# A transformer block on one core: image 0's output projection moved ahead of three V tiles and of image 1's P V, with P moves on a second queue

## The chip, the core and the metric

The kernel runs on one core of a Trainium2 chip. A core has a matrix engine (TensorE, PE), three engines for elementwise work (VectorE or DVE, ScalarE or ACT, GpSimd or POOL), SyncE (SP), which here only issues transfers, and 16 DMA engines that carry out what SP, ScalarE and GpSimd issue on their queues. Engines run their own instruction streams in order and wait for one another on semaphores. The metric is the device time of one execution in microseconds; less is better.

## The reference

Two images of 256 tokens, width 1152, two heads of 576, MLP width 4608, all bf16:

```
mod = (silu(c) @ w_mod).reshape(B, 6, 1, D)
shift_a, scale_a, gate_a, shift_m, scale_m, gate_m = [mod[:, i] for i in range(6)]
h = layernorm(x) * (1 + scale_a) + shift_a
q, k, v = split(h @ wqkv)                       # B, N, H, Dh
attn = softmax(einsum('bqhd,bkhd->bhqk', q, k) * Dh ** -0.5)
a = einsum('bhqk,bkhd->bqhd', attn, v).reshape(B, N, D) @ wo
x = x + gate_a * a
h2 = layernorm(x) * (1 + scale_m) + shift_m
out = x + gate_m * (gelu(h2 @ w_fc1) @ w_fc2)
```

## The kernel before

**Tiles.** The 512 tokens are four tiles t of 128; tiles 0 and 1 are image 0, tiles 2 and 3 image 1. The width is nine chunks of 128 (kt, or g for the attention output), or three column groups ci of 384. Everything lies in one SBUF array, "arena", cut by hand into regions that several buffers share in turn, and in eight PSUM banks.

**Stages on TensorE**, in order: modulation and LayerNorm 1, K, Q, the scores S of each image b and head h (index b*2+h), V (`v_proj(t, ci)`, nine matmuls of 384 columns, L1035), P V, the output projection (`wo_tile(t)`, three tiles of nine matmuls, L1164), FC1 (`fc1_tile(f, tok0, ntok)`, 36 rows f of the MLP width, nine matmuls of ntok columns each, L1205), FC2. A tile is evicted from PSUM by ScalarE or VectorE: `v_ev<t>_<ci>` on ScalarE, `wo_t1_<t>_<ci>` on VectorE (L1174), `gelu_<f>_<tok0>` on ScalarE (L1212).

**Softmax and the turn of P.** For each score block ScalarE makes the exponentials (`sexp`) and normalises (`spn`, L1026), VectorE turns P in 32 by 32 blocks (`PT_turn<idx>`, L1028), and four transfers of 32 KB put the turned blocks in place (`mv_pt<idx>_<a>`, L1030). Head 0 is idx 0 and 2, head 1 idx 1 and 3. Before, all sixteen are issued by SP.

**P V.** `pv(b, h)` (L1141) makes four chunks of one image and head in 16 matmuls of 256 columns and needs `PT` of that block; the chunk that holds the end of head 0 and the start of head 1 (g = 4) is made by `pv_halves()` (L1130) for both images, and needs all four. Results go to OT by `OT_ev<b>_<g>` and `OT_ev_4`. OT lies in the region of HX, which V's matmuls read. V itself lies in the region that later holds H2T, the normalised input of the MLP.

**The second LayerNorm.** After `wo_t1`, GpSimd adds x (`wo_x1`), VectorE takes statistics (`bn_ln2`), GpSimd finishes them (`rstd_ln2`, `nmr2`), ScalarE normalises (`xn2_<t>`, L1181), VectorE turns the tile (`h2turn_<t>`), four transfers move it (`mv_h2_<t>_<a>`), and nine pieces `h2T_<t>_<kt>` on ScalarE (L1199) and VectorE (L1202) apply scale and shift. FC1's first tiles use only the tokens that are ready: some rows f run first for 128 tokens (f < NF) or 256 (f < F0) and come back for the rest.

**Order.** TensorE's and SP's streams are in the order in which the program makes them; those of ScalarE, VectorE and GpSimd come from a list scheduler held by hand-written lists (`S.in_order`). The gates need a chain of their own on VectorE: `ga_<b>_<kt>` (16 operations of 1.41 us), which ends in `ga_t1`, and goes through a DRAM scratch to GA. `rows()` makes the MLP's shift and scale on TensorE, read by VectorE as `mt_0`, `mt_1`, `sc1m`. SP's large loads are W_O (`ld_wo`), the gate's and W_fc1's blocks of 512 columns (`ld_wfc1_<q>`, nine blocks in a ring of five slots), the MLP gate's weight (`ld_gm`) and four parts of W_fc2.

The order of the stage in question before:

```
        for t in range(1, 4):
            for ci in range(NCH):
                v_proj(t, ci)
...
        pv(0, 0)
        pv(1, 0)
        rows()
        pv_halves()
        pv(0, 1)
        pv(1, 1)
...
        wo_tile(0)
```

Of the kernel before, what the change touches and what calls it, by code (L numbers as in the profile page):

```python
# [515 lines left out]
NCH = 3  # L516
F0 = 20
NF = 10
KC = 5
# [33 lines left out]
def build_kernel(nc, x, c, wqkv, wo, w_mod, w_fc1, w_fc2, out):  # L553
# [5 lines left out]
    with (  # L559
# [70 lines left out]
        GM = [sb(o + 18432, 2304) for o in (O_A, O_C)]  # L630
        XN2 = [sb(O_R + 4 * W1 - (i + 1) * 2304, 2304) for i in range(4)]
        ACCA = sb(O_R, FG * 8, F32).rearrange("p (b d) -> p b d", b=2)
# [94 lines left out]

        def wfc1_load(q, k0=0, k1=KT):
            dma(WFC1[q % 5][:, k0:k1, :], wfc1_v[:, k0:k1, q * 512:(q + 1) * 512], (k1 - k0) * P * 1024, "ld_wfc1_%d_%d" % (q, k0), run=1024)

# [274 lines left out]
        def s_and_softmax(b, h):  # L1005
# [29 lines left out]
        def v_proj(t, ci):  # L1035
            bank = v_banks[v_rr[0] % 4]
            v_rr[0] += 1
# [89 lines left out]

        PVB = [(6, 7, 1, 6), (5, 2, 7, 5)]

        def pv_halves():  # L1130
            S.unit("pe", 4 * c_mm(256) + 100.0, "PV_halves")
            for b in range(2):
                for kjt in range(2):
                    for q in range(4):
                        r = slice(32 * q, 32 * q + 32)
                        mm(psum[r, b * 256:b * 256 + 256], V[:, 2 * b + kjt, 512 + 32 * q:544 + 32 * q],
                           PTS[b * 2 + q // 2][:, kjt], b == 0 and kjt == 0, b == 1 and kjt == 1, skip_group_check=True,
                           tile_position=(0, 32 * q))
            copy_on("act", OT[:, 4, :], ps32(0), 512, False, "OT_ev_4")

        def pv(b, h):  # L1141
# [13 lines left out]
        act(1500, lambda e: e.activation(out=SUMS[:, 0:1], in_=NHALF, func=ACTF.Gelu_apprx_tanh), [NHALF], [SUMS[:, 0:1]], "gelu_tab")  # L1155
        acc = [2, 3, 4, 6, 5, 7, 0, 1]
        acc_rr = [0]

        def acc_bank():
            b = acc[acc_rr[0] % len(acc)]  # L1160
            acc_rr[0] += 1
            return b

        def wo_tile(t):  # L1164
            b = t // 2
            for ci in range(NCH):
                S.unit("pe", KT * c_mm(CH), "wo_%d_%d" % (t, ci))
                o = ps32(acc_bank(), 0, CH)
                for g in range(KT):
                    mm(o, OT[:, g, t * 128:(t + 1) * 128], WO[:, g, ci * CH:(ci + 1) * CH], g == 0, g == KT - 1)  # L1170
                ga = GA[b][:, ci * CH:(ci + 1) * CH]
# [12 lines left out]

        TURNED = {0: H2F[3], 1: H2F[2], 2: XN2[0], 3: XN2[1]}

# [4 lines left out]
        def xn2_move(t):  # L1191
            b, b0 = t // 2, 0
            for a in range(4):
                dma(H2F[t][:, 288 * a:288 * a + 288], TURNED[t][32 * a:32 * a + 32, :], P * 576, "mv_h2_%d_%d" % (t, a), run=576, eng="act" if t in (0, 3) and a > 1 else "sp")
            for kt in range(KT):
                dst = H2T[:, kt, 4 * t:4 * t + 4, :]
                s1, s2 = SC1M[:, kt * 2 + b:kt * 2 + b + 1], SHM[:, kt * 32 + b:kt * 32 + b + 1]
                if kt < 7 if t == 0 else (kt > 6 if t == 1 else kt % 3 == 2):
                    act(330, lambda e, dst=dst, s1=s1, s2=s2: e.activation(out=dst, in_=dst, func=ACTF.Identity, scale=s1, bias=s2),  # L1199
# [5 lines left out]
        def fc1_tile(f, tok0, ntok):  # L1205
# [3 lines left out]
            for kt in range(KT):  # L1209
                mm(o, WFC1[q % 5][:, kt, (f % 4) * 128:(f % 4) * 128 + 128], H2T[:, kt, tok0 // 32:(tok0 + ntok) // 32, :], kt == 0, kt == KT - 1)  # L1210
            dst = GT[f][:, tok0:tok0 + ntok]
# [51 lines left out]
        wo_tile(2)  # L1263
# [12 lines left out]
        for f in (1, 2):  # L1276
            fc1_tile(f, 128, 256)
        for f in (1, 2):
            fc1_tile(f, 384, 128)
        fc1_tile(0, 256, 256)  # L1280
        for f in range(3, NF):
            fc1_tile(f, 128, 384)
        for f in range(NF, F0):
            fc1_tile(f, 256, 256)
        for f in range(F0, JT):
            if f % 4 == 0:
                if 24 <= f < 32:
                    wfc2_load(f // 4 - 5)
                wfc1_load(f // 4)
# [6 lines left out]
        for t in range(4):  # L1296
# [4 lines left out]
            for (c0, c1) in pieces:  # L1301
# [4 lines left out]
                for j in js:  # L1306
# [6 lines left out]

        S.n_other_dma_sems = 16
        small = ["ga_%s" % n for n in ("mv%d_1", "mv%d_2", "mv%d_3", "add%d_1", "add%d_3", "add%d_2", "bf%d", "t%d")]
        S.in_order("dve", ["ga_%d_%d" % (b, kt) for kt in range(3) for b in range(2)] + ["ga_0_%d" % kt for kt in range(3, 7)]
                   + ["smax_0", "snb_0", "ga_0_7", "sri_0", "ga_0_8", "smax_2", "snb_2", "PT_turn0", "smax_1", "snb_1", "sri_2", "ga_T0",
                      "smax_3", "snb_3", "sri_1", "PT_turn2", "ga_red0", "PT_turn1", "sri_3"] + [n % 0 for n in small] + ["PT_turn3"]
                   + ["ga_1_%d" % kt for kt in range(3, KT)] + ["ga_T1", "ga_red1"] + [n % 1 for n in small] + ["OT_ev0_7", "mt_0", "mt_1", "OT_ev1_7"])
        S.in_order("act", ["sexp_0_0", "sexp_0_1", "qk_ev8", "spn_0_0", "spn_0_1", "v_ev0_0", "sexp_2_0", "sexp_2_1", "sexp_1_0", "sexp_1_1", "v_ev0_1",  # L1320
                           "spn_2_0", "spn_2_1", "spn_1_0", "spn_1_1", "v_ev0_2", "sexp_3_0", "sexp_3_1", "v_ev1_0", "spn_3_0", "spn_3_1", "v_ev1_1", "v_ev1_2"])
        S.in_order("act", ["OT_ev0_0", "OT_ev0_2", "OT_ev1_0", "OT_ev1_2", "OT_ev_4", "OT_ev0_5", "OT_ev1_5", "gelu_tab", "xn2_0"])
        S.in_order("pool", ["wo_x1_0_0", "wo_x1_0_1", "wo_x1_0_2", "wo_x1_1_0", "rstd_ln2_0", "nmr2_0", "wo_x1_1_1", "wo_x1_1_2", "rstd_ln2_1", "nmr2_1", "wo_x1_2_0", "wo_x1_2_1", "wo_x1_2_2",
                            "wo_x1_3_0", "rstd_ln2_2", "nmr2_2", "wo_x1_3_1", "wo_x1_3_2", "rstd_ln2_3"])
# [55 lines left out]
```

## Time and profile before

| | |
|---|---|
| runs | 240.17 us (median of 3; 240.11 to 241.54) |
| the profiled execution | 240.14 us, of which the span of the profile is 238.2 us |
| TensorE busy in the span | 233.2 us, 1781 matmuls |
| VectorE, ScalarE, GpSimd busy | 125.7, 73.4, 23.4 us |
| granted TensorE clock | 1.0 |
| HBM read | 50.15 MB |

All times in this document that are positions are microseconds from the start of the span. The profile gives each engine's work in order of time (the timeline), in groups of like instructions by line, and in 40 equal slices; the chain that ended last, followed back from the end; the transfers, with the time from their issue to their landing; and what each engine waited for. "PE" is TensorE's matmuls, "PEld" its weight loads, "SPq" and "ACTq" the instructions by which SP and ScalarE issue a transfer. The chain's shares say what the end of the kernel depended on; an engine that is off the chain may wait at no cost.

### The profile page before, as it was taken

The numbers are of one execution on the slowest core, as the hardware profiler recorded it, in microseconds if no ns is written. First come the engines' busy times: TensorE is split into PE (matmuls) and PEld (weight loads), VectorE is DVE, ScalarE is ACT, GpSimd is POOL, SyncE is SP. The second block draws the span as 40 slices with busy tenths as digits, with TensorE's granted clock in tenths as the row PEclk, the third lists the DMA queues.
The fourth block names the chain that finished last, engine by engine and source line by source line (L and its number), as shares of the span: only waits on it lengthen the run. The fifth ranks groups of instructions, "written<-read, shape, count | busy, mean of one in ns | idle before, by whom it ended". The sixth has DMA issues, their size and how long they took to land.

```text
span 238.2 us, 4224 instructions
## 1 busy us (share of the span) xinstructions
PE 233.2 (98%) x1781; PEld 149.0 (63%) x1781; DVE 125.7 (53%) x233; ACT 73.4 (31%) x159; POOL 23.4 (10%) x48
## 2 busy tenths in 40 slices
PE   6899999999999999999999999999999999999995
PEld 2688844466667656989668644444665656656664
DVE  2654399979997699853299997000111111111112
ACT  4940540458535326767333333333000000000000
POOL 1300000000201467510000001100000000000000
DMA  6999999999999852849799999980000000000000
GB/s 219 361 372 391 352 391 391 394 412 410 316 355 356 259 190 63 256 112 318 242 385 371 390 354 379 392 313 2 3 17 17 19 17 17 17 22 23 22 20 18
DMA packets 36173, 53.31 MB, mean 224 GB/s; under 512 B 5371, under 2 KB 21627, under 8 KB 36155
## 3 DMA queue, kind: packets, MB, share of 16 engines
q1 hardware_dynamic: 34976, 51.85, 62.4%
q0 software_dynamic: 432, 0.89, 1.0%
q10 hardware_dynamic: 747, 0.31, 0.5%
q8 instruction: 14, 0.23, 0.4%
q14 instruction: 4, 0.03, 0.0%
HBM read 50.15 MB, written 1.19 MB: 216 GB/s over the span
## 4 chain that ended last, share of the span: by engine, by line
PE 95%; DMA 3%; SPq 1%; DVE 0%; issue 0%
PE psum L704 94%; DMA arena<-in_w_mod_dram 3%; SPq L685 1%; PE psum L707 0%; DVE arena L845 0%; DVE arena L1310 0%; DVE arena L1311 0%; DVE arena L833 0%
## 5 line engine op out<-in xcount | busy, mean ns | idle before, releaser
L704 PE MATMUL psum<-arena 128*128 128x384 bf16 (+10 forms) x1744 | 231.5, 302 | 2.1 <-POOL arena L732 1.5
L704 PEld LDWEIGHTS psum<-arena 128*128 128x128 bf16 (+3 forms) x1744 | 147.1, 97 | 84.8 <-issue 3.1
L1310 DVE TENSOR_TENSOR arena<-psum,arena 128x384 f32<-128x384 f32 (+2 forms) x13 | 6.8, 526 | 74.7 <-PE psum L704 74.7
L1212 ACT ACTIVATE arena<-psum 128x256 bf16<-128x256 f32 (+3 forms) x59 | 24.7, 430 | 41.2 <-PE psum L704 41.1
L699 ACT ACTIVATE arena<-psum 128x512 bf16<-128x512 f32 (+5 forms) x35 | 18.6, 561 | 30.8 <-PE psum L704 30.8
L1070 DVE SCALAR_TENSOR_TENSOR arena<-arena 128x1152 f32<-128x1152 bf16 x16 | 22.3, 1412 | 0.2
L1105 DVE SCALAR_TENSOR_TENSOR arena<-arena 128x1152 f32<-128x1152 bf16 x16 | 21.4, 1414 | 0.0
L685 POOL DMA_DIRECT2D dit_scratch<-arena x6 | 3.5, 584 | 99.5 <-DVE arena L1087 53.8
L754 DVE BATCH_NORM_STATS2 arena<-arena 128x6 f32<-128x384 f32 (+1 forms) x18 | 9.5, 549 | 4.1 <-DMA arena<-in_x_dram 3.9
L1175 POOL TENSOR_TENSOR arena<-arena 128x384 f32<-128x384 f32 x12 | 10.8, 912 | 5.9 <-DVE arena L1174 5.9
L1181 ACT ACTIVATE arena<-arena 128x1152 bf16<-128x1152 f32 x4 | 5.4, 1345 | 9.7 <-POOL arena L1180 6.4
L1174 DVE TENSOR_TENSOR arena<-psum,arena 128x384 f32<-128x384 f32 x12 | 6.5, 555 | 2.5 <-PE psum L704 2.5
L701 DVE CAST arena<-psum 128x512 bf16<-128x512 f32 x8 | 5.4, 684 | 4.1 <-PE psum L704 4.1
L1311 DVE TENSOR_TENSOR arena<-arena 128x384 bf16<-128x384 f32 (+2 forms) x13 | 6.9, 528 | 0.4
L1202 DVE TENSOR_SCALAR arena<-arena 128x128 bf16<-128x128 bf16 x21 | 5.4, 326 | 3.0 <-DMA arena<-arena 3.0
L1199 ACT ACTIVATE arena<-arena 128x128 bf16<-128x128 bf16 x15 | 6.2, 482 | 0.1
L1189 DVE STREAM_TRANSPOSE arena<-arena 128x1152 bf16<-128x1152 bf16 x4 | 5.5, 1377 | 1.1 <-ACT arena L1181 1.1
L1102 DVE TENSOR_SCALAR arena<-arena 128x1152 f32<-128x1152 bf16 x2 | 1.6, 818 | 7.6 <-DMA arena<-in_w_mod_dram 7.6
L1021 ACT ACTIVATE arena<-psum,arena 128x256 bf16<-128x256 f32 x8 | 3.7, 469 | 2.4 <-DVE arena L1018 1.9
L758 POOL TENSOR_TENSOR arena<-arena 128x1 f32<-128x1 f32 x6 | 3.4, 566 | 3.8 <-DVE arena L757 3.6
L1026 ACT ACTIVATE arena<-arena 128x256 bf16<-128x256 bf16 x8 | 3.6, 501 | 0.1
L1017 DVE TENSOR_REDUCE arena<-psum 128x2 f32<-128x512 f32 x4 | 2.8, 690 | 1.5 <-PE psum L704 1.3
(64 smaller groups left out, 62.0 us busy)
## 6 DMA issues: line engine op xcount, KB each, us to landing
arena<-in_w_fc_dram SPq DMA_DIRECT2D x4, 2592.0 KB, 17.2
arena<-in_w_fc_dram SPq DMA_DIRECT2D x8, 1152.0 KB, 12.0
arena<-in_w_mod_dram SPq DMA_DIRECT2D x6, 864.0 KB, 11.4
arena<-in_w_mod_dram SPq DMA_DIRECT2D x3, 1728.0 KB, 20.4
arena<-in_wqkv_dram SPq DMA_DIRECT2D x9, 288.0 KB, 8.0
arena<-in_wqkv_dram SPq DMA_DIRECT2D x1, 2592.0 KB, 18.2
arena<-in_wo_dram SPq DMA_DIRECT2D x1, 2592.0 KB, 9.8
arena<-in_w_mod_dram SPq DMA_DIRECT2D x1, 2592.0 KB, 11.0
```

What stands on the lines that cost most here:

```text
L685: return S.op(eng, 500.0 if eng == "sp" else 150.0, lambda e: e.dma_start(dst, src), reads=[src], writes=[dst], name=name, dma_bytes=nbyte ...
L699: act(c_act(n), lambda e: e.activation(out=dst, in_=src, func=ACTF.Copy), [src], [dst], name)
L704: S.instr(lambda e: e.matmul(o, lhsT=l, rhs=r, start=st, stop=sp, **kw), reads=[l, r], writes=[o])
L754: dve(550, lambda e, s=s, o=o: e.bn_stats(out=o, in_=s), [s], [o], "bn_%s_%d" % (tag, ci))
L1070: ga_units[(b, kt)] = dve(150 + FG * 1.1, lambda e, o=o, w=w, s1=s1: e.scalar_tensor_tensor(out=o, in0=w, scalar=s1, in1=o, op0=ALU.mult, ...
L1105: u = dve(1300, lambda e, o=o, w=w, s1=s1: e.scalar_tensor_tensor(out=o, in0=w, scalar=s1, in1=o, op0=ALU.mult, op1=ALU.add), [w, s1, o], ...
L1174: dve(550, lambda e, o=o, ga=ga, x1c=x1c: e.tensor_tensor(out=x1c, in0=o, in1=ga, op=ALU.mult), [o, ga], [x1c], "wo_t1_%d_%d" % (t, ci))
L1175: S.op("pool", 930, lambda e, xs=xs, x1c=x1c: e.tensor_tensor(out=x1c, in0=x1c, in1=xs, op=ALU.add), reads=[x1c, xs], writes=[x1c], name=" ...
L1199: act(330, lambda e, dst=dst, s1=s1, s2=s2: e.activation(out=dst, in_=dst, func=ACTF.Identity, scale=s1, bias=s2), [dst, s1, s2], [dst], " ...
L1212: act(c_act(ntok), lambda e: e.activation(out=dst, in_=o, func=ACTF.Gelu_apprx_tanh), [o], [dst], "gelu_%d_%d" % (f, tok0))
L1310: dve(c_dve_psum32(w), lambda e, o=o, gm=gm, t1=t1: e.tensor_tensor(out=t1, in0=o, in1=gm, op=ALU.mult), [o, gm], [t1], "fc2_t1_%d_%d" % ( ...
L1311: dve(c_dve_32(w), lambda e, t1=t1, x1c=x1c, ost=ost: e.tensor_tensor(out=ost, in0=t1, in1=x1c, op=ALU.add), [t1, x1c], [ost], "fc2_out_%d ...
```

## The change

Image 0's six W_O tiles come ahead of three of V's tiles (3_0, 2_2, 3_2) and of image 1's P V. Both heads of image 0 are multiplied before `rows`. The moves of P for head 1 (idx 1 and 3) are issued by ScalarE instead of SP. The result of `pv_halves` gets a buffer of its own, OT4, where Q4B was, so that it doesn't overwrite HX; two turned tiles of the second LayerNorm get room too. W_fc1's ring has four slots instead of five, block 3 is loaded in one piece, and blocks 2 and 3 are issued after the moves of tiles 0 and 1. FC1's split is another: 3 rows start with 128 tokens, 8 with 256, 3 with 384, and from row 14 on all 512 go at once (before: 10 rows at 128, 10 at 256, 512 from row 20). The PSUM banks and the hand-written orders of ScalarE and VectorE follow; ScalarE does 20 of the 36 `h2T` pieces instead of 15.

```diff
-F0 = 20
-NF = 10
+NF = 3
+F1 = 11
+F0 = 14
...
-        WFC1 = [wmat(o, 512) for o in (O_A, O_A + 9216, O_C, O_C + 9216, O_R + 3 * W1)]
+        WFC1 = [wmat(o, 512) for o in (O_A, O_A + 9216, O_C, O_C + 9216)]
...
+        OT4 = sb(O_Q4B, 1024)
...
-                dma(PPF[idx][:, 128 * a:128 * a + 128], flat[32 * a:32 * a + 32, :], P * 256, "mv_pt%d_%d" % (idx, a), run=256)
+                dma(PPF[idx][:, 128 * a:128 * a + 128], flat[32 * a:32 * a + 32, :], P * 256, "mv_pt%d_%d" % (idx, a), run=256, eng="act" if h else "sp")
...
-        PVB = [(6, 7, 1, 6), (5, 2, 7, 5)]
+        PVB = [(6, 5, 1, 2), (1, 2, 0, 7)]
...
-            copy_on("act", OT[:, 4, :], ps32(0), 512, False, "OT_ev_4")
+            copy_on("act", OT4, ps32(0), 512, False, "OT_ev_4")
...
-            for i, eng in ((0, "act"), (1, "dve" if h else "act")):
+            for i, eng in ((0, "act" if h or not b else "dve"), (1, "dve" if b and h else "act")):
...
-                dma(H2F[t][:, 288 * a:288 * a + 288], TURNED[t][32 * a:32 * a + 32, :], P * 576, "mv_h2_%d_%d" % (t, a), run=576, eng="act" if t in (0, 3) and a > 1 else "sp")
+                dma(H2F[t][:, 288 * a:288 * a + 288], TURNED[t][32 * a:32 * a + 32, :], P * 576, "mv_h2_%d_%d" % (t, a), run=576, eng="act" if t > 2 and a > 1 else "sp")
...
         v_proj(0, 2)
-        for t in range(1, 4):
-            for ci in range(NCH):
-                v_proj(t, ci)
-        wfc1_load(2)
+        for ci in range(NCH):
+            v_proj(1, ci)
+        v_proj(2, 1)
+        v_proj(3, 1)
+        v_proj(2, 0)
         gate_load(1)
-        wfc1_load(3, 0, 7)
         pv(0, 0)
-        pv(1, 0)
+        pv(0, 1)
         rows()
         pv_halves()
-        pv(0, 1)
-        pv(1, 1)
...
         wo_tile(0)
+        wo_tile(1)
+        v_proj(3, 0, 7)
+        v_proj(2, 2, 6)
+        v_proj(3, 2, 5)
+        pv(1, 0)
+        pv(1, 1)
         xn2_turn(0)
         xn2_move(0)
-        wo_tile(1)
+        wfc1_load(2)
         xn2_turn(1)
         xn2_move(1)
-        wfc1_load(3, 7, KT)
-        wfc1_load(4)
+        wfc1_load(3)
         wo_tile(2)
...
-        fc1_tile(0, 128, 128)
-        for f in range(NF, F0):
+        for f in range(NF, F1):
             fc1_tile(f, 0, 256)
+        for f in range(F1, F0):
+            fc1_tile(f, 0, 384)
         mlp_gate(last_h2T[0])
...
+        for f in range(NF):
+            fc1_tile(f, 128, 384)
+        for f in range(NF, F1):
+            fc1_tile(f, 256, 256)
+        for f in range(F1, F0):
+            fc1_tile(f, 384, 128)
```

In the built program ScalarE's stream from `v_ev1_0` on is: v_ev1_0, mv_pt1_0, spn_3_0, mv_pt1_1, spn_3_1, mv_pt1_2, v_ev1_1, mv_pt1_3, v_ev1_2, v_ev2_1, mv_pt3_0 to mv_pt3_3, v_ev3_1, v_ev2_0, the four OT_ev0 copies, OT_ev_4, gelu_tab, xn2_0, v_ev3_0, v_ev2_2, v_ev3_2, OT_ev1_2, OT_ev1_5, xn2_1, the h2T pieces of tile 0 and five of tile 1, xn2_2, gelu_0 to gelu_6, xn2_3, three pieces of tile 2, gelu_7, gelu_8, mv_h2_3_2, mv_h2_3_3, gelu_9 to gelu_11, three pieces of tile 3. SP's stream is: the moves of head 0, ld_wo, ld_wfc1_0, ld_wfc1_1, the gate of image 1, the moves of tile 0, ld_wfc1_2, the moves of tile 1, ld_wfc1_3, the moves of tile 2, two of tile 3, ld_gm, and the rest of the weights.

More of the change, by code (lines that the diff above doesn't have):

```diff
@@ L630, in build_kernel @@
         GM = [sb(o + 18432, 2304) for o in (O_A, O_C)]
-        XN2 = [sb(O_R + 4 * W1 - (i + 1) * 2304, 2304) for i in range(4)]
+        XN2 = [sb(O_R + 4 * W1 - (i + 1) * 2304, 2304) for i in range(6)]
         ACCA = sb(O_R, FG * 8, F32).rearrange("p (b d) -> p b d", b=2)
@@ L726, in build_kernel, with wfc1_load @@
             dma(WK[:, k0:k1, 1024:D], wqkv_v[:, k0:k1, D + 1024:2 * D], (k1 - k0) * P * 256, "ld_wkl%d" % k0, run=256)
-        def wfc1_load(q, k0=0, k1=KT):
-            dma(WFC1[q % 5][:, k0:k1, :], wfc1_v[:, k0:k1, q * 512:(q + 1) * 512], (k1 - k0) * P * 1024, "ld_wfc1_%d_%d" % (q, k0), run=1024)
+        def wfc1_load(q):
+            dma(WFC1[q % 4], wfc1_v[:, :, q * 512:(q + 1) * 512], D * 512 * 2, "ld_wfc1_%d" % q, run=1024)
         S.op("pool", 100, lambda e: e.memset(ONES, 1.0), writes=[ONES], name="ones")
@@ L1029, in s_and_softmax, with v_proj @@
             for a in range(4):
-                dma(PPF[idx][:, 128 * a:128 * a + 128], flat[32 * a:32 * a + 32, :], P * 256, "mv_pt%d_%d" % (idx, a), run=256)
+                dma(PPF[idx][:, 128 * a:128 * a + 128], flat[32 * a:32 * a + 32, :], P * 256, "mv_pt%d_%d" % (idx, a), run=256, eng="act" if h else "sp")
         v_banks = [7, 0, 1, 2]
         v_rr = [0]
-        def v_proj(t, ci):
-            bank = v_banks[v_rr[0] % 4]
-            v_rr[0] += 1
+        def v_proj(t, ci, bank=None):
+            if bank is None:
+                bank = v_banks[v_rr[0] % 4]
+                v_rr[0] += 1
             S.unit("pe", KT * c_mm(CH), "v_%d_%d" % (t, ci))
@@ L1155, in build_kernel @@
         act(1500, lambda e: e.activation(out=SUMS[:, 0:1], in_=NHALF, func=ACTF.Gelu_apprx_tanh), [NHALF], [SUMS[:, 0:1]], "gelu_tab")
-        acc = [2, 3, 4, 6, 5, 7, 0, 1]
-        acc_rr = [0]
+        acc = [3, 4, 6, 5, 1, 2, 0, 7]
+        acc_rr = [-12]
         def acc_bank():
-            b = acc[acc_rr[0] % len(acc)]
+            b = (7, 6, 5, 1, 2, 0, 6, 5, 1, 2, 0, 7)[acc_rr[0]] if acc_rr[0] < 0 else acc[acc_rr[0] % len(acc)]
             acc_rr[0] += 1
@@ L1169, in wo_tile @@
                 for g in range(KT):
-                    mm(o, OT[:, g, t * 128:(t + 1) * 128], WO[:, g, ci * CH:(ci + 1) * CH], g == 0, g == KT - 1)
+                    mm(o, OT4[:, t * 128:(t + 1) * 128] if g == 4 else OT[:, g, t * 128:(t + 1) * 128], WO[:, g, ci * CH:(ci + 1) * CH], g == 0, g == KT - 1)
                 ga = GA[b][:, ci * CH:(ci + 1) * CH]
@@ L1183, in build_kernel @@
         last_h2T = [None]
-        TURNED = {0: H2F[3], 1: H2F[2], 2: XN2[0], 3: XN2[1]}
+        TURNED = {0: XN2[4], 1: XN2[5], 2: XN2[0], 3: XN2[1]}
         def xn2_turn(t):
@@ L1197, in xn2_move @@
                 s1, s2 = SC1M[:, kt * 2 + b:kt * 2 + b + 1], SHM[:, kt * 32 + b:kt * 32 + b + 1]
-                if kt < 7 if t == 0 else (kt > 6 if t == 1 else kt % 3 == 2):
+                if t == 0 or (kt < 5 if t == 1 else kt % 3 == 2):
                     act(330, lambda e, dst=dst, s1=s1, s2=s2: e.activation(out=dst, in_=dst, func=ACTF.Identity, scale=s1, bias=s2),
@@ L1209, in fc1_tile @@
             for kt in range(KT):
-                mm(o, WFC1[q % 5][:, kt, (f % 4) * 128:(f % 4) * 128 + 128], H2T[:, kt, tok0 // 32:(tok0 + ntok) // 32, :], kt == 0, kt == KT - 1)
+                mm(o, WFC1[q % 4][:, kt, (f % 4) * 128:(f % 4) * 128 + 128], H2T[:, kt, tok0 // 32:(tok0 + ntok) // 32, :], kt == 0, kt == KT - 1)
             dst = GT[f][:, tok0:tok0 + ntok]
@@ L1271, in build_kernel @@
             fc1_tile(f, 0, 128)
-        fc1_tile(0, 128, 128)
-        for f in range(NF, F0):
+        for f in range(NF, F1):
             fc1_tile(f, 0, 256)
+        for f in range(F1, F0):
+            fc1_tile(f, 0, 384)
         mlp_gate(last_h2T[0])
-        for f in (1, 2):
-            fc1_tile(f, 128, 256)
-        for f in (1, 2):
-            fc1_tile(f, 384, 128)
[L1280 to L1284, printed above, removed]
+        for f in range(NF):
[3 more added lines that the diff above has]
+        for f in range(F1, F0):
+            fc1_tile(f, 384, 128)
         for f in range(F0, JT):
-            if f % 4 == 0:
+            if f % 4 == 0 and f >= 16:
                 if 24 <= f < 32:
@@ L1312, in build_kernel @@
                 dma(outv[b, :, t % 2, c0:c1], ost, P * w * 2, "st_out_%d_%d" % (t, c0), is_out=True)
-        S.n_other_dma_sems = 16
+        S.n_other_dma_sems = 22
         small = ["ga_%s" % n for n in ("mv%d_1", "mv%d_2", "mv%d_3", "add%d_1", "add%d_3", "add%d_2", "bf%d", "t%d")]
@@ L1318, in build_kernel @@
                       "smax_3", "snb_3", "sri_1", "PT_turn2", "ga_red0", "PT_turn1", "sri_3"] + [n % 0 for n in small] + ["PT_turn3"]
-                   + ["ga_1_%d" % kt for kt in range(3, KT)] + ["ga_T1", "ga_red1"] + [n % 1 for n in small] + ["OT_ev0_7", "mt_0", "mt_1", "OT_ev1_7"])
+                   + ["ga_1_%d" % kt for kt in range(3, KT)] + ["ga_T1", "ga_red1"] + [n % 1 for n in small])
         S.in_order("act", ["sexp_0_0", "sexp_0_1", "qk_ev8", "spn_0_0", "spn_0_1", "v_ev0_0", "sexp_2_0", "sexp_2_1", "sexp_1_0", "sexp_1_1", "v_ev0_1",
@@ L1321, in build_kernel @@
                            "spn_2_0", "spn_2_1", "spn_1_0", "spn_1_1", "v_ev0_2", "sexp_3_0", "sexp_3_1", "v_ev1_0", "spn_3_0", "spn_3_1", "v_ev1_1", "v_ev1_2"])
-        S.in_order("act", ["OT_ev0_0", "OT_ev0_2", "OT_ev1_0", "OT_ev1_2", "OT_ev_4", "OT_ev0_5", "OT_ev1_5", "gelu_tab", "xn2_0"])
+        S.in_order("act", ["OT_ev0_0", "OT_ev0_2", "OT_ev0_5", "OT_ev0_7", "OT_ev_4", "gelu_tab", "xn2_0"])
         S.in_order("pool", ["wo_x1_0_0", "wo_x1_0_1", "wo_x1_0_2", "wo_x1_1_0", "rstd_ln2_0", "nmr2_0", "wo_x1_1_1", "wo_x1_1_2", "rstd_ln2_1", "nmr2_1", "wo_x1_2_0", "wo_x1_2_1", "wo_x1_2_2",
@@ L1324, in build_kernel @@
                             "wo_x1_3_0", "rstd_ln2_2", "nmr2_2", "wo_x1_3_1", "wo_x1_3_2", "rstd_ln2_3"])
-        S.in_order("dve", ['wo_t1_0_0', 'wo_t1_0_1', 'bn_ln2_0_0', 'wo_t1_0_2', 'bn_ln2_0_1', 'wo_t1_1_0', 'bn_ln2_0_2', 'aggr_ln2_0', 'veps_ln2_0', 'wo_t1_1_1', 'bn_ln2_1_0', 'wo_t1_1_2', 'bn_ln2_1_1', 'h2turn_0', 'bn_ln2_1_2', 'aggr_ln2_1', 'veps_ln2_1', 'wo_t1_2_0', 'wo_t1_2_1', 'wo_t1_2_2', 'bn_ln2_2_0', 'h2turn_1', 'h2T_0_7', 'h2T_0_8', 'wo_t1_3_0', 'bn_ln2_2_1', 'bn_ln2_2_2', 'aggr_ln2_2', 'veps_ln2_2', 'wo_t1_3_1', 'wo_t1_3_2', 'bn_ln2_3_0', 'h2T_1_0', 'h2T_1_1', 'h2T_1_2', 'h2T_1_3', 'h2T_1_4', 'h2T_1_5', 'h2T_1_6', 'bn_ln2_3_1', 'bn_ln2_3_2', 'aggr_ln2_3', 'veps_ln2_3', 'h2turn_2', 'h2turn_3'])
@@ L1326, in build_kernel @@
-        S.in_order("act", ['xn2_0', 'xn2_1', 'h2T_0_0', 'h2T_0_1', 'h2T_0_2', 'h2T_0_3', 'h2T_0_4', 'h2T_0_5', 'h2T_0_6', 'gelu_0_0', 'gelu_1_0', 'gelu_2_0', 'gelu_3_0', 'xn2_2', 'h2T_1_7', 'h2T_1_8', 'gelu_4_0', 'gelu_5_0', 'gelu_6_0', 'gelu_7_0', 'gelu_8_0', 'gelu_9_0'])
+        S.in_order("dve", ["ga_t1", "wo_t1_0_0", "wo_t1_0_1", "wo_t1_0_2", "bn_ln2_0_0", "wo_t1_1_0", "bn_ln2_0_1", "bn_ln2_0_2", "aggr_ln2_0", "veps_ln2_0",
[4 rows of a table added]
+        S.in_order("act", ["xn2_0", "v_ev3_0", "v_ev2_2", "v_ev3_2", "OT_ev1_2", "OT_ev1_5", "xn2_1"] + ["h2T_0_%d" % kt for kt in range(KT)] + ["h2T_1_%d" % kt for kt in range(5)] + ["xn2_2"])
@@ L1331, in build_kernel @@
             sems = {e: es.enter_context(nc.semaphore("c_" + e)) for e in ENGINES}
-            dma_sems = [es.enter_context(nc.semaphore("d%d" % i)) for i in range(70)]
+            dma_sems = [es.enter_context(nc.semaphore("d%d" % i)) for i in range(76)]
             S.emit(nc, block, sems, dma_sems)
```

4 rows, old and new, of the table small are left out of this document.

## The prediction

> **What bounds the kernel now.** I read the page's busy times, then the chain that ended last.
>
> ```profile
> PE 233.2 (98%) x1781; PEld 149.0 (63%) x1781; DVE 125.7 (53%) x233; ACT 73.4 (31%) x159; POOL 23.4 (10%) x48
> ...
> DMA  6999999999999852849799999980000000000000
> ```
>
> ```profile
> by line: PE psum L704 94.1%; DMA arena<-in_w_mod_dram 2.9%; SPq L685 0.9%; PE psum L707 0.5%; issue 0.2%; DVE arena L845 0.1%; DVE arena L1310 0.1%; DVE arena L1311 0.1%; DVE arena L833 0.0%
> ...
> 16.23 219.47 PE psum L704 x1643
> ```
>
> From 16.23 to 235.70 us TensorE waits for nothing that is seen. A busy share could still hide short waits, so I took its pace from ScalarE's timeline, where each gelu starts as its FC1 tile of nine matmuls ends (128 columns in the first two rows, 512 in the others).
>
> ```profile
> 95.50 0.28 ACT L1212 ACTIVATE arena<-psum 128x128 bf16<-128x128 f32 x1 [0.72 <-PE psum L704]
> 96.00 0.28 ACT L1212 ACTIVATE arena<-psum 128x128 bf16<-128x128 f32 x1 [0.22 <-PE psum L704]
> ...
> 136.30 0.60 ACT L1212 ACTIVATE arena<-psum 128x512 bf16<-128x512 f32 x1 [1.56 <-PE psum L704]
> 138.25 0.60 ACT L1212 ACTIVATE arena<-psum 128x512 bf16<-128x512 f32 x1 [1.35 <-PE psum L704]
> ```
>
> The steps are 0.50 and 1.95 us, so 56 and 216 ns a matmul. With the steps of 256 columns (125.52 to 126.50) and 384 (123.07 to 124.53), 109 and 162 ns, all four lie on one line: 0.417 ns a column and 2.5 ns fixed. TensorE is full in every stage after 16 us, and the change leaves all before that alone. A reordering has no stall to remove; it can only drop matmuls or make stalls. So I look for what TensorE will meet too early.
>
> Three transfers matter, on SP's timeline, with the times to landing below (W_O's own, then that of the last P move, issued at 66.51).
>
> ```profile
> 60.62 0.59 SPq L685 DMA_DIRECT2D arena<-in_wo_dram  x1
> 61.26 5.88 SPq L685 DMA_DIRECT2D arena<-arena  x8
> ```
>
> ```profile
> arena<-in_wo_dram SPq DMA_DIRECT2D x1, 2592.0 KB, 9.8
> ```
>
> ```profile
> arena<-arena SPq DMA_DIRECT2D x1, 32.0 KB, 5.7
> ```
>
> W_O lands at 60.62 + 9.8 = 70.4 and the last of the eight head-1 moves behind it at 72.2, though issued long before: the queue is saturated (DMA slices at 9). Eight moves cost that stream 1.8 us.
>
> **Term 1, matmuls: -0.2.** FC1 keeps its 36 x 512 columns for each of nine chunks, but the tiles fall from 59 (13 of 128, 23 of 256, 7 of 384, 16 of 512) to 50 (6, 16, 6, 22). 81 matmuls fewer at 2.5 ns fixed. Nothing else on TensorE changes in number.
>
> **Term 2, W_O is needed 6 us earlier: +0.95.** V's eviction of tile 1_2 starts at 62.32 in both. Before, six tiles more follow, the last evicted at 71.10; after, three: 2_1, 3_1, 2_0, at 1.46 us, to 66.71. Then come PV_0_0 and PV_0_1 (0.87 us each, as 71.10 to 71.97), rows and PV_halves (from 72.84, where PV_1_0 must end, to 76.57 less PV_0_1's 0.87: 2.86). That is 71.31 on the evictions' clock, and TensorE issues some 0.2 us ahead of it: wo_0_0 could start at 71.1. W_O is still issued after the head-0 moves, at 60.62. The head-1 moves, now on ScalarE's queue, run while it flows. If they cost it nothing it lands at 70.4 and there is no stall; if they cost all they cost behind it, 72.2 and 1.1. They are issued between 60 and 68, before W_O ends, so I take the upper end less a move: 72.0, a wait of 0.95. [...] No run so far shows such moves beside a full queue.
>
> **Term 3, ScalarE now issues eight moves: +0.1.** Its own issues are these, with their landing:
>
> ```profile
> L685 ACTq DMA_DIRECT2D arena<-arena x4: 578/646/836, 88.7 to 105.4; - x4
> ...
> DMA to landing us min/median/max: 2.2/2.5/4.1
> ```
>
> In the built program its order from 60.04 (v_ev1_0's end) to v_ev3_1 is: eight issues of x, two spn (0.91), three V evictions (3 x 0.49), and v_ev3_1 itself (0.49); back to back they overlap by about 0.3, so v_ev3_1 ends at 62.6 + 8x. PV_0_1's third group writes bank 2, which that eviction frees: 66.5 + 0.87 + 0.44 = 67.8. The wait is 8x - 5.2: nothing at 0.65, 0.4 at 0.70, 1.5 at 0.84. Up to 0.95 it is the same wait as term 2's, only sooner. With a median of 0.646 I book 0.1; to 1.0 for 0.84. Queued behind these issues are also spn_3_1 and so PT_turn3, which starts about 1 us late, and with it the gate chain on VectorE (ga_t1 from 75.2 to about 76.2) and wo_t1_0_0. That is covered: the six W_O tiles of image 0 have six banks, and TensorE first needs one back at v_3_0, near 81. Without that cover, 1 us. The moves themselves must land by 67.4 (PV_0_1) and 70.5 (PV_halves): the last is issued near 67, and 2.5 to 4.1 us give 69.5 to 71.1, inside term 2's wait; POOL's stores in this stage took 5.3, and with that 1.8 us would show.
>
> **Term 4, the P V evictions of image 1 just ahead of wo_2_0: +0.1.** VectorE's OT_ev1_0 (0.65 to 0.69) can start when PV_1_0 ends and must be done one P V unit, 0.87, later less TensorE's lead of 0.2. 0 to 0.2. PV_halves' own copy is hidden behind W_O: before, OT_ev_4 came 0.5 after the unit's end, so with 0.6 of copy it would show 0.45 in wo_0_0's fifth matmul were W_O on time.
>
> **Term 5, the second LayerNorm of image 1 must be ready sooner: +0.3.** Tokens 384 to 511 are first used by fc1_1_384, 17.3 us after FC1 begins, and are ready 2.1 us ahead (VectorE's last L1202 group ends at 109.97). After, fc1_0_128 uses them after 3 tiles of 128, 8 of 256 and 3 of 384: 1.5 + 7.9 + 4.4 = 13.8 us. The chain: gelu_6 ends 6.0 us after FC1 begins (3 x 0.50 + 4 x 0.98 + 0.2 + 0.38), xn2_3 (1.35) and h2turn_3 (1.38) bring it to 8.7; two of its four moves wait on ScalarE for h2T_2's three pieces and two gelus, about 1.3; then as before 3.8 from turn to first piece, and 0.3 for that: 14.1. A stall of 0.3; 0 to 0.9 by landings of 2.2 to 3.1. fc1_11_0 has about 0.2 in hand on h2T_2.
>
> **Priced at nothing.** Four W_fc1 blocks instead of five: block 4, landed at 103.5 before, now waits for its slot until about 115 and moves the loads behind it some 4 us later; the last, W_fc2's, landed at 161.4 and is needed near 169.6, W_fc1's seventh has 6 us. Without that cover each us late is a us. xn2_0 ahead of v_ev3_0 on ScalarE: 7.0 us after wo_t1_0_0 at most (78.91 to 85.93), so 83.3 and the eviction by 85.1, as PV_1_0 wants it. W_fc1's blocks 0 and 1 go to SP's queue 6 us sooner, behind W_O, where nothing waits for them. Room, banks and the split of h2T cost no time by themselves.
>
> **Sum.** -0.2 + 0.95 + 0.1 + 0.1 + 0.3 = +1.25. The profiled execution took 240.14 (span 238.2 and 1.9 around it), the median 240.17: about **241.4**. Term by term it runs from -0.2 to +3.0 (-0.2 + 1.1 + 1.0 + 0.2 + 0.9), 239.9 to 243.1.
>
> **Rivals.**
> Everything is ready: W_O is not slowed by the moves and lands at 70.4, and the last chain makes it. Then only term 1 and small change are left, 240.0. For it: the moves are 0.26 MB beside W_O's 2.65; against it: DMA slices at 9 just there. It is also the best case, since TensorE's columns are fixed.
> ScalarE's issues are held up: slower. SP's issues took 0.54 to 1.19 for the same move and up to 6.0 for a W_fc1 block when its queue was deep:
>
> ```profile
> L685 SPq DMA_DIRECT2D arena<-arena x28: 543/603/1194, 54.1 to 105.9; - x28
> ...
> L685 SPq DMA_DIRECT2D arena<-in_w_fc_dram x14: 367/844/6042, 67.2 to 140.7; - x14
> ```
>
> Now SP has W_O and two W_fc1 blocks queued from 61 on. If that depth holds ScalarE's issues too, the place is v_ev3_1 and the price 8x - 5.2, with 0.45 for OT_ev_4 now uncovered and terms 1, 4, 5: 2.4 us at 0.87 each, 5.0 at 1.19, which gives 245.1. Against it: ScalarE's four took 0.58 to 0.84, but beside a nearly empty queue.
> Weights late in FC1 through the four slots: 2 to 3 us if the loads after 115 us slip 8 instead of 4: 243.
>
> **How the numbers follow.** Forecast 0.55 (its own range 240.3 to 242.6), everything ready 0.15, held-up issues 0.25, late weights 0.05. About 1%, 2.4 us, is what a measurement of this kernel can tell from no change. Faster by that is ruled out by the full TensorE but for surprise, 0.01. Within: most of the forecast's 0.55, the 0.15 and a little, 0.68. Slower: 0.31. The range goes from 239.8 to 245.3.
>
> **What would show it.** TensorE's first wait after 16 us stands in front of wo_0_0, about 1 us, released by in_wo_dram, with W_O's landing near 11.4 us; the ACTq issues of arena<-arena near 0.65; one more wait of some tenths at about 110 us, released by VectorE L1205. A wait on ScalarE L701 near 68 us of over 1.5 us means the held-up issues; no wait at all, the first rival. Wrong altogether would be a loss with no wait in TensorE's rows, or under 239.

## The result, and the profile after

The changed kernel takes **242.56 us** (median of six runs, 242.5 to 244.24; the kernel before 240.14, 240.07 to 241.54, beside it): ratio 1.0101, 95% interval 1.0067 to 1.0136. The profiled execution took 242.5 with a span of 240.4; before, the span was 238.2, so 2.2 us have to be found. One of the six executions ran at a mean granted clock of 0.993 and took 244.24; the other five, at 0.999 to 1.0, took 242.5 to 242.64.

The page's busy times, its DMA slices and the costliest group (its last columns are the idle time in front of it and what ended most of that):

```profile
PE 233.1 (97%) x1700; PEld 143.5 (60%) x1700; DVE 124.0 (52%) x228; ACT 74.2 (31%) x155; POOL 23.5 (10%) x48
...
DMA  6999999999999237539799999993000000000000
...
L706 PE MATMUL psum<-arena 128*128 128x384 bf16 (+9 forms) x1663 | 231.6, 308 | 4.5 <-DMA arena<-arena 1.6
```

TensorE has 81 matmuls fewer, and a new wait of 1.6 us, released by a transfer inside the core (arena to arena): a move of P, not W_O. The DMA engines are full until 78 us as they were before, so through all of this. The chain that ended last shows which (start, length, what):

```profile
62.25 6.82 DMA arena<-arena
69.07 0.14 issue
69.21 4.27 PE psum L706 x98
73.48 0.59 ACT arena L701
74.07 0.05 issue
74.12 163.84 PE psum L706 x1065
```

Before, one piece of 219.47 us stood here from 16.23 on. Now the chain goes through the move issued at 62.25, mv_pt1_3, the fourth of head 1, image 0; it lands 6.82 us after its issue. PV_0_1 starts on that at 69.21; PV_0_0 (a `pv` is eight matmuls of 256 columns, not 16) had started its last matmul at 67.32, and 0.11 is a matmul's pace at 256 columns, so TensorE lost 69.21 - 67.32 - 0.11 = **1.78 us** there. (The 1.6 in the page's row is the same wait: it counts from the modelled end of that matmul, 0.16 later.) The second break, at 73.48, is OT_ev_4's copy: **0.54 us** lost inside wo_0_0, by the same reckoning. Another 0.08 is lost ahead of wo_2_0, for OT_ev1_0. With 0.2 fewer for the 81 matmuls: 1.78 + 0.54 + 0.08 - 0.2 = 2.2, the whole difference of the spans.

ScalarE's timeline has the issues, and the list of DMA issues the medians from issue to landing:

```profile
62.25 0.73 ACTq L687 DMA_DIRECT2D arena<-arena  x1
...
63.83 2.57 ACTq L687 DMA_DIRECT2D arena<-arena  x4
66.45 0.87 ACT L701 ACTIVATE arena<-psum 128x384 bf16<-128x384 f32 x2 [2.13 <-PE psum L706]
```

```profile
arena<-in_wo_dram SPq DMA_DIRECT2D x1, 2592.0 KB, 10.6
...
arena<-arena ACTq DMA_DIRECT2D x8, 32.0 KB, 6.4
```

The issues took 0.55 to 0.82 us, so ScalarE was not held up; the landings were slow. The trace has the eight at 64.25, 67.08, 68.08, 69.07, 70.07, 71.06, 71.48 and 72.04: a gap after the first, and then one microsecond a move. W_O landed at 71.25, while wo_0_0 began at 72.92.

### The profile page after: what moved, and what is told of

Read it like the earlier page. It is cut to its first block, busy times and chain, and to the rows that moved or that the text cites. A ratio compares the mean times of both kernels' runs of the same rounds, so it can differ in the third digit from the quotient of the medians.

```text
span 240.4 us, 4048 instructions
## 1 busy us (share of the span) xinstructions
PE 233.1 (97%) x1700; PEld 143.5 (60%) x1700; DVE 124.0 (52%) x228; ACT 74.2 (31%) x155; POOL 23.5 (10%) x48
## 4 chain that ended last, share of the span: by engine, by line
PE 90%; DMA 5%; DVE 2%; ACT 1%; issue 0%; SPq 0%; ACTq 0%
PE psum L706 89%; DMA arena<-arena 3%; DMA arena<-in_w_mod_dram 2%; PE psum L709 1%; DVE arena L1030 1%; DVE arena L1080 1%; ACT arena L1028 0%; SPq L687 0%; DVE arena L1019 0%; ACT arena L701 0%; DVE arena L1083 0%; ACTq L687 0%; DVE arena L847 0%; DVE arena L1314 0%; DVE arena L1315 0%
## 5 line engine op out<-in xcount | busy, mean ns | idle before, releaser
L706 PE MATMUL psum<-arena 128*128 128x384 bf16 (+9 forms) x1663 | 231.6, 308 | 4.5 <-DMA arena<-arena 1.6
L706 PEld LDWEIGHTS psum<-arena 128*128 128x128 bf16 (+2 forms) x1663 | 141.4, 97 | 93.0 <-issue 3.1
L1215 ACT ACTIVATE arena<-psum 128x512 bf16<-128x512 f32 (+3 forms) x50 | 23.1, 474 | 39.1 <-PE psum L706 38.8
L1202 ACT ACTIVATE arena<-arena 128x128 bf16<-128x128 bf16 x20 | 8.1, 480 | 5.3 <-DMA arena<-arena 5.3
L1205 DVE TENSOR_SCALAR arena<-arena 128x128 bf16<-128x128 bf16 x16 | 3.8, 308 | 3.5 <-DMA arena<-arena 3.5
```

The costliest lines, as they stand in the source:

```text
L706: S.instr(lambda e: e.matmul(o, lhsT=l, rhs=r, start=st, stop=sp, **kw), reads=[l, r], writes=[o])
L1215: act(c_act(ntok), lambda e: e.activation(out=dst, in_=o, func=ACTF.Gelu_apprx_tanh), [o], [dst], "gelu_%d_%d" % (f, tok0))
```

## The experiments

**Theory.** A small move that is in flight beside W_O's stream on another queue is slowed by sharing the 16 DMA engines, and the P V of head 1 now comes before the slowed moves are in. **Rivals.** ScalarE's issues or ScalarE's queue by itself are the cost; or SP's deep queue is.

**One part undone: the moves back on SP.**

```diff
-... "mv_pt%d_%d" % (idx, a), run=256, eng="act" if h else "sp")
+... "mv_pt%d_%d" % (idx, a), run=256, eng="sp")
```

> The changed kernel with one part undone: the eight head-1 moves of P are issued by SP again, behind W_O, as before the change; everything else (W_O needed early, the reordered V and P V) stays. Theory: the queue is the cause. TensorE's 1.78 us wait ahead of PV_0_1 is the time at which a move lands that shares the DMA engines with W_O; behind W_O the moves land as they did before the change, the first four by 71.5 us from the span's start and the last by 72.3. PV_0_1 would then wait until about 71.6, 4.2 us instead of 1.8, and the sum is 242.6 + 2.4, less what the later waits lose by it: 244.5 to 245.1. Rival: moves on ScalarE's queue are themselves the cost (its eight issues and a slow queue); then taking them off it gives the time back, 240.5 to 241.

Measured: 246.76 us (ratio 1.0284, 1.0253 to 1.0315). Its chain, and busy time with granted clock by stage (after the stage come its length and PE's busy time; the clock is the number ahead of the last two):

```profile
64.03 7.28 DMA arena<-arena
...
71.44 6.82 PE psum L706 x88
```

```profile
66.00:69.00 3.00, 1.62 (x13) 1.01 (x11) 2.93 (x3) 1.58 (x3) 0.50 (x1) 1.00 1.05 399
69.00:71.40 2.40, 0.00 (x0) 0.00 (x0) 2.33 (x3) 0.00 (x0) 0.08 (x1) 0.81 1.18 287
71.40:74.00 2.60, 2.56 (x24) 1.52 (x28) 2.50 (x4) 0.66 (x2) 0.00 (x0) 0.50 1.07 362
74.00:77.00 3.00, 3.00 (x56) 1.73 (x52) 1.08 (x7) 0.43 (x1) 1.03 (x2) 0.50 1.09 349
77.00:80.00 3.00, 2.85 (x41) 1.57 (x32) 0.04 (x1) 1.70 (x2) 0.00 (x0) 0.95 0.44 134
```

Behind W_O in one queue the fourth move lands at 71.31 and TensorE loses 3.98 us ahead of PV_0_1, as the theory had it. The change's own queue is thus better than the old one for this order. The expected total was some 2 us too low, for a reason that no theory had: after the idle time the granted clock is 0.50 until about 77.3 (0.95 over the last stage is half speed for its first 0.3 us), and the matmuls of PV_0_1, the rows and PV_halves took twice as long (213 instead of 109 ns at 256 columns). From PV_0_1's start to wo_0_0's it is 6.52 us instead of 3.71, so 2.8 more. In the profiled execution of the changed kernel, with 1.78 us of idle time, the clock stayed at 1.00. With the moves back on SP it fell 3.0 us after TensorE had stopped (0.81 over 2.4 us is half speed for the last 0.9) and came back after 5.9 us of work.

The stretch at half speed is 6.8 us long here (70.5 to 77.3), and 6.8 us too in the two other traces that have one: 76.6 to 83.4 with W_O out of the way, 71.6 to 78.5 with the queues swapped (both below). The waits in front of them differ (3.98, 8.25 and 3.63 us). In this kernel it cost about half of the part that fell on work (2.8 of 5.9 us). It doesn't come out alike each time: two of this kernel's four executions had a mean clock of 0.986 and took 247.2 and 248.0 us, the other two 0.993, so about half as long at half speed, and 246.3.

**One part alone: the moves on ScalarE's queue, in the kernel before.** The same edit the other way round, with eight more semaphores for the landings.

> The kernel before, with one part of the change alone: the eight head-1 moves of P go on ScalarE's queue. TensorE's order stays that of before, so PV_0_1 needs the moves after 75 us and PV_1_0's neighbours need them no earlier than 70.9. Theory: the moves are slow beside W_O in any order of TensorE's work: they land about 1.0 us apart between 64 and 72 us, 6 us and more after issue, and W_O lands about 0.8 us later (near 71.2), but nothing waits: 240.0 to 240.4. Rival: ScalarE's eight issues, some 5.2 us of its time, cost by themselves (late V evictions): 0.5 us and more, 240.7 to 242.

Measured: 240.15 us (ratio 1.0001, 0.9992 to 1.001).

```profile
16.02 219.48 PE psum L704 x1643
```

```profile
arena<-in_wo_dram SPq DMA_DIRECT2D x1, 2592.0 KB, 11.0
...
arena<-arena ACTq DMA_DIRECT2D x8, 32.0 KB, 6.4
```

The moves are as slow (6.4 us; landings 64.2 to 71.9), ScalarE issues as many, and TensorE has its unbroken piece. The issues cost nothing, and the slow moves cost nothing where P V comes late. So it is the new order of TensorE that makes the moves' landings cost something, on either queue: 1.78 us ahead of PV_0_1 with the moves on ScalarE's, 3.98 with them on SP's.

**SP's queue less deep.** W_fc1's blocks 0 and 1 issued after the gate's load of image 1.

> The changed kernel, with the loads of W_fc1's blocks 0 and 1 issued only after the last V unit that stands ahead of P V, not right behind W_O. SP's queue then holds W_O alone while the head-1 moves are in flight. Theory A, turn about with W_O alone: the spacing of the moves stays about 1.0 us, because each of their packets waits for one of W_O's, and TensorE's wait ahead of PV_0_1 stays 1.5 to 1.9 us: 242.3 to 242.7. Theory B, a deep queue on SP holds the moves up (the second to fourth moves were issued by 63.0 us and no packet of theirs is seen from 63.5 to 64.5): they start at once, the fourth lands 1 to 1.5 us sooner, near 67.8, and the wait falls to 0.3 to 0.8: 241.1 to 241.6.

Measured: 242.38 us (1.0092, 1.0075 to 1.0109). The moves land at 64.38, 67.02, 68.10, 69.01, then 70.02 to 72.06, as in the changed kernel, and the wait ahead of PV_0_1 is 1.93 us. Theory A: W_O alone is enough.

**W_O out of the way.** W_O on ScalarE's queue behind the eight moves, W_fc1's blocks held as above.

```diff
-        dma(WO, wo_v, D * D * 2, "ld_wo", run=2304)
+        dma(WO, wo_v, D * D * 2, "ld_wo", run=2304, eng="act")
...
-... "v_ev1_1", "v_ev1_2"])
+... "v_ev1_1", "v_ev1_2", "v_ev2_1", "mv_pt3_0", "mv_pt3_1", "mv_pt3_2", "mv_pt3_3", "ld_wo", "v_ev3_1", "v_ev2_0", "OT_ev0_0"])
```

> The changed kernel, with W_O's load moved to ScalarE's queue behind all eight head-1 moves, and the first two W_fc1 loads issued after the gate's load: the eight moves then have no other load of SP's beside them once the loads ahead of W_O are through (near 63 us). It is a probe of the moves; W_O is late by this. Theory: W_O's stream is what makes a move take 1.0 us; without it they land as they are issued, 0.55 to 0.8 us apart and 2.2 to 3.5 us after their issue, and PV_0_1 waits for nothing. Rival: ScalarE's queue takes 1 us for each such move beside anything or nothing; then they land 1.0 us apart as before. The time itself, by theory: W_O issued near 66.4 and landing 9 to 10 us later, a wait of 4.5 to 5 us ahead of wo_0_0 in place of 1.78 + 0.54, and, if TensorE's clock is halved behind a wait of that length as it was behind 3.98 us, 2.6 more: 244.8 to 248.

Measured: one execution of 250.28 us. From its DMA issues and TensorE's waits:

```profile
arena<-arena ACTq DMA_DIRECT2D x8, 32.0 KB, 2.5
```

```profile
PE psum L706 <- DMA arena<-in_wo_dram: 8.1, 1, 8.1
```

The same issues, at the same times, on the same queue, now land after a median of 2.5 us instead of 6.4 (the fourth at 65.27 instead of 69.07), and nothing waits ahead of PV_0_1. So ScalarE's queue is not slow; W_O's stream makes it so. The time itself came out over the expected one because W_O took 12.8 us from issue to landing and not 9 to 10. The clock was at 0.50 again (76.6 to 83.4) behind the wait, as the expectation had reckoned with.

**The queues swapped.** W_O issued by ScalarE (after sexp_3_1), all sixteen moves by SP.

> The changed kernel with the two queues swapped: W_O's load is issued by ScalarE (near 59.7 us) and all sixteen moves of P by SP, the first two W_fc1 loads behind them. Theory: it is the sharing of the DMA engines between two queues that makes a move slow, whichever queue it is on: the head-1 moves on SP's queue land 0.9 to 1.1 us apart and 5 to 7 us after issue beside W_O, and PV_0_1 waits 1.2 to 2.2 us: 242 to 243. Rival: ScalarE's queue itself is the slow one; on SP's queue the moves land 0.2 to 0.65 us apart, PV_0_1 waits for nothing, and with OT_ev_4's 0.5 left it is 240.6 to 241.2.

Measured: 247.85 us (1.0313, 1.0291 to 1.0335). TensorE's timeline (idle time and releaser in brackets), and the packets of the two queues from 63 to 67 us (q1 is SP's, q10 ScalarE's; packets, MB, share of the engines):

```profile
67.95 1.03 PE L706 MATMUL psum<-arena 128*128 128x256 bf16 x8 [1.14 <-DMA arena<-arena]
72.45 3.88 PE L706 MATMUL psum<-arena 128*128 128x256 bf16 x40 [3.47 <-DMA arena<-arena]
```

```profile
q10 hardware_dynamic: 577, 1.33, 90.7%
q1 hardware_dynamic: 576, 0.13, 17.0%
```

Now the moves on SP's queue are slow: those of image 1's head 0, for example, land 1.0 us apart (68.65, 69.63, 70.66). Whichever queue they are on, they share. The expected size was wrong, since all sixteen moves had to pass beside or behind W_O and not eight, so that PV_0_0 waited too and PV_0_1 3.5 us, with the clock at 0.50 (71.6 to 78.5) behind it. The same count in the changed kernel, from 65 to 69 us:

```profile
q1 hardware_dynamic: 605, 1.39, 90.9%
q10 hardware_dynamic: 542, 0.13, 15.2%
```

In both, one packet of the moves' queue passes for about one of W_O's 2304-byte packets (of the 542 and 576, 492 and 512 are 256 bytes long, the rest 4). A move of 32 KB in packets of 256 bytes is eight packets for each of the 16 engines, and 8 x (0.1 + 0.02) us, by the packets' own times in the trace (96 and 19 ns on average in the changed kernel), is the microsecond between landings.

**Shorter packets for W_O,** in two loads of half rows and in four of quarter rows.

```diff
-        dma(WO, wo_v, D * D * 2, "ld_wo", run=2304)
+        for c in range(2):
+            dma(WO[:, :, c * 576:(c + 1) * 576], wo_v[:, :, c * 576:(c + 1) * 576], D * D, "ld_wo%d" % c, run=1152)
```

> The changed kernel, with W_O in two loads of 576 columns each instead of one of 1152: the same bytes, in packets of 1152 bytes instead of 2304. Theory: the moves' 256-byte packets go turn about with W_O's, one for one, so a move's time is 8 packets per DMA engine times the sum of both packets' times, near 8 x (0.1 + 0.02) us; with half the bytes in W_O's packets the spacing of the moves falls from 1.0 us to 0.5 to 0.7, the fourth lands near 67.8, and the wait ahead of PV_0_1 falls to 0.3 to 0.8. W_O is held up the more and lands 0.5 to 1 us later, near 72, about when it is needed: 241 to 242. Rival: the moves' 5 to 7 us are a latency of ScalarE's queue that W_O's packets have no part in; then spacing, wait and time stay, 242.4 to 242.8.

> The changed kernel, with W_O in four loads of 288 columns, so packets of 576 bytes instead of 2304 (1152 in the run with halves). Theory A, shares by bytes or time: the moves get one 256-byte packet for each 2.3 KB or 0.1 us of W_O whatever W_O's packet size, so they stay 0.9 to 1.1 us apart, the first after the gap comes as early as with halves or earlier, and PV_0_1 waits 0.4 to 0.9: 241.2 to 241.7 if W_O is in time. Theory B, turns by packets: with packets a quarter as long a move's turn comes four times as often, the spacing falls to 0.3 to 0.6 and the wait to 0: 240.9 to 241.2. In both W_O may be the later for its small packets: past 72 us on its landing takes the wait over in front of wo_0_0, to 242 at 73.

Measured: halves 241.53 us (1.0062, 1.0047 to 1.0077), quarters 241.03 (1.0036, 1.0023 to 1.005). Packets from 65 to 69 us, of the halves and then of the quarters:

```profile
q1 hardware_dynamic: 1196, 1.36, 94.3%
q10 hardware_dynamic: 615, 0.14, 16.3%
```

```profile
q1 hardware_dynamic: 2092, 1.19, 102.3%
q10 hardware_dynamic: 413, 0.09, 11.1%
```

The times went about where expected, but turns of one packet for one, the reason given for the halves and Theory B of the quarters, were not it. They would have given the moves more packets; they got 615 and 413 in the 4 us, against 542: about one for each 2.2 to 2.9 KB of W_O in all three. That is nearer to the quarters' Theory A (shares by bytes or time), though 241.03 lies in the other theory's range. The landings stayed near 1 us apart with halves (66.29, 67.51, 68.24, 69.26). What got better is the gap after the first move: the second landed at 66.29 and 65.65 instead of 67.08, the fourth at 68.24 and 67.82 instead of 69.07, and the wait ahead of PV_0_1 fell to 0.76 and 0.33. In the quarters the moves' packets come in bunches, the first of them just ahead of the landing of W_O's first part (65.88), the next around that of its second (68.16). The counts of whole rows (605 of W_O to 542 of the moves) fit turns of one for one; those of halves (1.9 to 1) and quarters (5.1 to 1) do not, and what sets the ratio, and the gap after the first move, stays open.

**The half-copies used last.** In image 0's projection, the chunks in the order 0, 1, 2, 3, 5, 6, 7, 8, 4.

> The changed kernel, with the nine matmuls of image 0's output projection tiles taken in the order 0, 1, 2, 3, 5, 6, 7, 8, 4: the chunk that comes from OT_ev_4's copy is used last, four matmuls (0.65 us) later. Theory: the 0.54 us wait inside wo_0_0 is OT_ev_4, bare because TensorE's wait lies ahead of PV_0_1 and not ahead of wo_0_0; it goes: 242.56 - 0.54 = 242.0 (241.9 to 242.1), and nothing else moves. Rival: W_O or another eviction is late just behind it, and the wait only changes its name: 242.3 to 242.6.

Measured: 242.26 us (1.0097, 1.0068 to 1.0126), which alone can't be told from the changed kernel. The chain tells it:

```profile
69.77 168.20 PE psum L706 x1165
```

From PV_0_1's start on the piece is unbroken, and from there to the span's end it takes 170.6 us (240.4 - 69.77) where the changed kernel takes 171.2 (240.4 - 69.21). The 0.54 is gone; this execution had come to PV_0_1 0.56 later, by its slower start (the first move was issued at 60.48 and not 59.99).

**Two orders that give the moves time.** The first puts V's tiles 3_0 and 2_2 ahead of P V, 3_2 between the projection's tiles, and the half-copies last.

> A version that keeps the change and gives the moves time: V's tiles 3_0 and 2_2 go ahead of P V (2.9 us of matmuls that need no P), V's tile 3_2 stands between the output projection's tiles of image 0, and the chunk of OT_ev_4 is used last. Theory: PV_0_1 starts near 70.3, after the fourth move's landing (69.1), PV_halves after the eighth (72.0), wo_0_0 after W_O (71.3): all three waits go, 242.56 - 1.78 - 0.54 = 240.2, 240.0 to 240.4. That is the time before less the 0.2 of the fewer matmuls, so no more than the same within what is measured. Rival: the later output projection meets a new wait (VectorE's evictions ahead of PV_1_0, or xn2_0 for the MLP): 240.8 to 242.

Measured: 243.75 us (1.0156, 1.0129 to 1.0184). Three of its six executions had a mean granted clock of 0.993 and took 244.5 to 244.7; the other three took 242.7 to 243.0, so it is no better than the change, and slower by 0.1 to 0.5 where the clock was full. TensorE waits for no move any more, but 2.8 us ahead of wo_2_0, for OT_ev1_0 on VectorE:

```profile
85.86 1.38 DVE L1193 STREAM_TRANSPOSE arena<-arena 128x1152 bf16<-128x1152 bf16 x1
...
88.05 1.28 DVE L703 CAST arena<-psum 128x512 bf16<-128x512 f32 x2
```

PV_1_0 ended near 85.3, and its copy stands in VectorE's order behind the second LayerNorm of image 0 (h2turn_0 at 85.86 and three smaller operations). The V tiles that the change left between the projection and image 1's P V are what VectorE needs to get through that; in the changed kernel it was free 1.5 us ahead. The rival was named, its price set too low.

The second order moves only V's tile 3_0 and the rows unit ahead of PV_0_1, keeps 2_2 and 3_2 where they were, half-copies last.

```diff
         v_proj(2, 0)
+        v_proj(3, 0)
         gate_load(1)
         pv(0, 0)
-        pv(0, 1)
         rows()
+        pv(0, 1)
...
-        v_proj(3, 0, 7)
-        v_proj(2, 2, 6)
+        v_proj(2, 2, 7)
```

> The changed kernel with TensorE's order mended a second way: one V tile (3_0) and the rows unit go ahead of PV_0_1, two V tiles (2_2 and 3_2) stay between image 0's output projection and image 1's P V, and the chunk of OT_ev_4 is used last for image 0. Theory: PV_0_1 starts near 71.1 us, after the fourth move (69.1), PV_halves near 72.2, after the eighth (72.0), wo_0_0 after W_O (71.3); and VectorE, which in the version with V first reached OT_ev1_0 2.8 us too late, keeps two V tiles of time for the LayerNorm work ahead of it: its slack was 1.5 us with three tiles, so 0 to 0.3 now. 242.56 - 1.78 - 0.54 + 0.2 = 240.4, 240.1 to 240.7. Rival: VectorE's queue is late again, by 0.6 to 1.5: 241 to 241.9.

Measured: 240.36 us (1.0006, 0.9993 to 1.0019).

```profile
16.11 219.58 PE psum L706 x1562
```

TensorE's unbroken piece is back, with the moves as slow as ever (landings 66.78 to 71.94) and W_O at 71.70. So the two waits named above are the whole loss. Nothing beats the kernel before by what can be measured: the one gain in the change, fewer matmuls, is 0.2 us.

## Why the prediction was right, and where it was not

The time (241.4 forecast, 242.56 measured) lies at the upper end of the forecast's own range (240.3 to 242.6), and by luck: the waits that it booked were hardly paid, and the one that was paid stands in front of another unit, for another transfer.

**What bounds it** held: TensorE had no stall to give back, and every loss is a wait.

**Term 1, -0.2:** right. From fc1_0_0's first matmul to fc2_0_0's the trace has 70.45 us before and 70.24 after.

**Term 2, +0.95, a wait for W_O:** not paid. The moves, now beside W_O, held it up by 0.8 us (70.47 to 71.25), not by 1.55. wo_0_0 could have begun at 72.92 - 1.78 = 71.14, as predicted (71.1), so some 0.2 would have shown; it hid behind the earlier wait.

**Term 3, +0.1:** its first half was near enough (0.1 booked, nothing paid). The eight issues took 0.66 us each on average, v_ev3_1 ended at 66.94 and stopped nothing, and the rival of held-up issues fell: SP's own issues of W_fc1's two blocks took 1.5 and 5.2 us beside them. **The step that failed is its last sentence,** the landing of the moves. It reckoned 2.5 to 4.1 us for the last move, from ScalarE's four moves at 88 to 105 us, where the DMA slices of the page before stand at 2 to 8, and put the rest inside term 2's wait. The fourth move, which PV_0_1 needs at 67.4, got no sum of its own; beside W_O it took 6.8 us from 62.25. The prediction asked what the moves do to W_O, and hardly what W_O does to the moves: 0.8 us the one way, 3.8 us the other (the fourth move landed at 69.07, and at 65.27 with W_O out of the way). It did have a row of small transfers beside the full stream, POOL's stores at 5.3 us, and gave 1.8 us as their price, but booked nothing for it. That this is the size of the loss is chance: the 1.8 was for the last move, ahead of PV_halves; for the fourth, 62.25 + 5.3 is 67.55, a wait of under 0.2.

**OT_ev_4, "0.45 were W_O on time":** right in size (0.54) and wrong in cover, since the wait stands ahead of PV_0_1, two units earlier, and hides nothing of what follows PV_halves.

**Term 4, +0.1:** 0.08.

**Term 5, +0.3:** nothing. h2turn_3 ended 8.8 us after FC1's start (106.01 and 97.25; 8.7 predicted), and its first piece was made 4.8 us later, not 5.4. The 1.3 us in which two moves were to wait on ScalarE was not paid: ScalarE's two were issued at 106.04 and 106.66, as SP's were (106.04 and 106.62). But ScalarE's second landed 3.75 us after its issue, more than the 2.2 to 3.1 reckoned, so the two errors partly cancel. The pieces came from 110.85 on, and fc1_0_128 began at 111.00.

**The other rivals.** Everything ready (240.0): not so, though the last version comes within 0.4 of it. Late weights in FC1: no wait of TensorE after wo_2_0, so four slots were enough.

So +1.25 against 2.2 in the span: terms 2, 3 and 5 were 1.35 and came to nothing, and 2.3 came from one landing and from the cover that went with it.

## What to carry to other kernels

When a transfer is moved to another queue to get it past a long one, price it by a row in which such a transfer runs beside a full stream, not by its landing on a quiet chip; and ask it for the first piece that somebody needs, not for the last. An overlap that hides one step ("behind W_O's wait") is gone when an earlier wait takes that one's place, so price each such step bare as well. Work that stands between two stages on the bounding engine may be there for a slower neighbour: look up how far ahead that neighbour is before it is moved.

## What was not expected of the hardware

A wait of TensorE can cost more than its length: in the profiled executions 1.78 and 1.93 us of idle time left the granted clock at 1.00, while 3.98, 8.25 and 1.30 + 3.63 us brought a stretch of 6.8 us at 0.50, of which 4 to 6 us fell on work, 2.8 us more in the first case. The shorter waits are not shown to be safe: one execution in six of the changed kernel and three in six of the version with a wait of 2.8 us had a mean clock of 0.993 and took about 1.7 us longer. But one in fifteen of the kernel before, which has no such wait, shows the same (0.993 and 241.69 us, 1.5 longer, measured beside the last version), so the cause of these stays open. And cutting the large load's rows into shorter packets gave the small transfers little more of the engines or even less (615 and 413 packets against 542), but it did let them start sooner, for 0.8 us (halves) to 1.2 us (quarters) on the fourth move's landing.
